# VectorE's order from pair 10 on, and second MLP steps in one piece, in an attention-then-MLP kernel on one core

## The chip, the core and the metric

The kernel runs on one core of a Trainium2 chip. A core has five engines with a queue of instructions each: TensorE (PE, matrix products), VectorE (DVE), ScalarE (ACT), GpSimd (POOL) and SyncE (SP, which here only issues DMAs). They wait for one another by semaphores; within an engine instructions run in the order of its queue. SBUF is the working memory of 128 partitions; PSUM holds TensorE's results, in banks. The metric is the device time of one execution in microseconds, lower is better.

## The reference, cut to what matters

```python
# q, k, v: (8 batches, 8 heads, 576 positions, 64); factor 4
q_d, k_d, v_d = means of q, k, v over groups of 4 positions      # 144 positions
out_d   = softmax(q_d k_d^T / 8) v_d                             # coarse attention
out_up  = out_d, each row repeated 4 times
out_loc = softmax(q k^T / 8 where |i - j| < 4) v                 # local attention
x = (out_up + out_loc) as (4608 tokens, 512)
h = x @ w_in                                                     # 512 -> 2048
out = (h * sigmoid(h)) @ w_out                                   # 2048 -> 512
```

## The kernel before

Attention runs over 32 pairs of heads (`NPAIR`), the MLP over 9 blocks `j` of 512 tokens. Each piece of work is a *unit* with a name, an engine and an estimated cost. A planner (`Plan.order`, L252) puts the units of each engine in order: first those that are written out by hand in `FIRST` (L164), then, whenever an engine is free in its model, the ready unit with the lowest priority value. A unit made without a priority gets its number in order of making.

For one pair p the units are:

- `T{p}` (PE, L600): transposes q and k into the PSUM banks o0 and pe_. `eq{p}` copies q out of o0 (`qT`, ScalarE up to pair 11, VectorE from 12 on, L396), `ek{p}` copies k out of pe_ (ScalarE, L616), `mk{p}` and `mq{p}` make the sums over 4 positions (VectorE, L620 and L624).
- `S{p}` (PE, L636): scores into bank pair AB. `x{p}` and `xd{p}` (ScalarE, L658 and L660) take the exponentials; `x{p}` also releases later loads of q, k and v on SP (`tick`). `k{p}` (VectorE, L662) multiplies by the band mask.
- `Z{p}` (PE): row sums into CD. `r{p}` (VectorE, three instructions, L771, L772, L774) adds the two halves and takes reciprocals; `z{p}` and `b{p}` (DMAs issued by ScalarE, L776 and L779) send them to HBM and back, spread as `Rb`.
- `PV{p}` (PE): products with v into CD. `m{p}` (VectorE, four instructions, L809 to L812) multiplies by `Rb` into `xo`; `a{p}` (GpSimd, L836) adds coarse and local parts into `xT`, the MLP's input.
- GpSimd also casts what is loaded: `va`, `cw`, `vb`, `c` (L593, L588, L595, L578).

From pair 10 on, T of pair n+1, S of pair n, PV of n-2 and Z of n-1 are one TensorE unit, `V{n}` (L902).

The MLP has two kinds of steps. `g1_{j}_{f}` (L841) is 4 matmuls into one half of bank pair HP; `t{j}_{f}` (ScalarE, tanh, L850) and `s{j}_{f}` (VectorE, L852) make 128 columns of the gated hidden layer `gT` of it and free the half. `g2_{j}_{tt}_{part}` (L858) is 4 of the 16 matmuls that make 128 rows of the output in o0 or pe_; after part 3, `o{j}_{tt}` (ScalarE, L867) copies them out and SP stores them. So bank o0 is shared: T writes it, `eq` reads it, then g2 writes it, `o` reads it, and T of the next step follows.

The last loop (L986) makes one `V`, four g1 and one g2 of four parts a step; from there on the planner's choice follows priorities, as `FIRST` ends in the steps V10 to V12.

Of the kernel before, what the change touches and what calls it, by code (L numbers as in the profile page):

```python
# [15 lines left out]
NPAIR = B_ * H_ // 2  # L16
# [3 lines left out]
NDIR = 10  # L20
# [131 lines left out]
class Unit:  # L152
# [5 lines left out]
    def __init__(self, eng, name, cost, prio, dcost=0.0):  # L158
# [7 lines left out]
        T0 T1 S0 T2 S1 Z0 VP0 T3 Z1 RB0 PV0 VP1 S2 T4 PV1 RB1 Z2 VP2 S3 T5 PV2 Z3 RB2 VP3 S4 T6 PV3 RB3 Z4  # L166
        VP4 S5 T7 Z5 RB4 VP5 PV4 g1_0_0 g1_0_1 S6 T8 g1_0_2 g1_0_3 RB5 Z6 g1_0_4 S7 g1_0_5 PV5 VP6 g1_0_6
        RB6 T9 Z7 g1_0_7 g1_0_8 S8 PV6 VP7 g1_0_9 g1_0_10 RB7 T10 Z8 g1_0_11 g1_0_12 S9 PV7 VP8 g1_0_13
        g1_0_14 RB8 g1_0_15 g1_1_0 g1_1_1 V10 g1_1_2 g1_1_3 VP9 g2_0_0_0 g2_0_0_1 g2_0_0_2 RB9 g2_0_0_3
        g1_1_4 g1_1_5 V11 g1_1_6 g1_1_7 VP10 g2_0_1_0 g2_0_1_1""",  # L170
    "ACT": """
        lkx lk0 ckx eq0 ek0 cw0 eq1 ek1 cw1 x0 xd0 eq2 ek2 x1 xd1 ev0 rh0 eq3 ek3 eb0 rh1 ev1 x2 xd2 eq4 ek4
        eb1 rh2 ev2 x3 xd3 eq5 ek5 eb2 rh3 ev3 x4 xd4 eq6 ek6 eb3 rh4 ev4 x5 xd5 eq7 ek7 eb4 rh5 ev5 t0_0
        t0_1 x6 xd6 eq8 t0_2 t0_3 eb5 ek8 rh6 t0_4 x7 xd7 t0_5 ev6 t0_6 eb6 eq9 ek9 rh7 t0_7 t0_8 x8 xd8 ev7
        t0_9 t0_10 eb7 eq10 ek10 rh8 t0_11 t0_12 x9 xd9 ev8 t0_13 t0_14 eb8 t0_15 t1_0 t1_1 eq11 ek11 rh9
        t1_2 t1_3 x10 xd10 ev9 eb9 o0_0 t1_4 t1_5 ek12 x11 z10 t1_6 t1_7 xd11""",
    "DVE": """
        const const.1 const.2 const.3 const.4 const.5 const.6 const.7 const.8 const.9 const.11 const.10
        const.12 const.14 const.13 const.15 const.16 const.17 const.18 const.19 const.20 const.21 const.22
# [2 lines left out]
        mk2 r0 k1 rx0 rm0 rl0 r1 mk3 m0 rx1 rm1 rl1 k2 r2 mk4 rx2 m1 rm2 k3 rl2 r3 mk5 m2 rx3 rm3 rl3 k4 r4  # L182
        mk6 rx4 m3 rm4 k5 rl4 r5 mk7 rx5 m4 rm5 rl5 s0_0 s0_1 k6 mq8 s0_2 r6 s0_3 mk8 rx6 s0_4 rm6 k7 rl6 m5
        s0_5 s0_6 r7 mq9 mk9 rx7 s0_7 rm7 s0_8 rl7 k8 m6 s0_9 s0_10 r8 mq10 mk10 rx8 s0_11 rm8 s0_12 rl8 k9
        m7 s0_13 s0_14 s0_15 s1_0 s1_1 r9 m8 mk11 rx9 s1_2 rm9 s1_3 rl9 mq11 k10 s1_4 s1_5 r10 eq12 mk12
        mq12 s1_6""",
    "POOL": """
        const.28 const.31 const.29 const.32 const.30 const.33 const.34 const.35 const.36 const.66 const.69
        const.42 const.43 const.44 const.45 const.46 const.47 const.48 const.49 const.50 const.51 const.52
        const.53 const.54 const.55 const.56 const.57 const.58 const.59 const.60 const.61 mq0 c2 mq1 c3 mq2  # L190
        cw2 c4 w0 cw3 mq3 c5 a0 cw4 mq4 w1 c6 a1 cw5 mq5 a2 w2 c7 cw6 mq6 a3 c8 cw7 w3 a4 mq7 c9 cw8 w4 c10
        w5 a5 w6 cw9 w7 a6 a7 c11 cw10 c12 cw11 cw12 c13 a8 a8.1 a8.2 c14 cw13""",
    "SP": """
        lq0 lq1 lk1 lv0.1 lv0.2 lv0.3 lq2 lv0e lv0 lk2 lv1 lv1.1 lv1.2 lv1.3 lq3 lk3 lv2 lv2.1 lv2.2 lv2.3
        lq4 lk4 lv3 lv3.1 lv3.2 lv3.3 lq5 lk5 lv4 lv4.1 lv4.2 lv4.3 lq6 lk6 lv5 lv5.1 lv5.2 lv5.3 lq7 lk7
        lv6 lv6.1 lv6.2 lv6.3 lq8 lk8 lv7 lv7.1 lv7.2 lv7.3 lq9 lk9 lv8 lv8.1 lv8.2 lv8.3 lq10 lk10 lv9
        lv9.1 lv9.2 lv9.3 lq11 lk11 lv10 lv10.1 lv10.2 lv10.3 lv11 lv11.1 lv11.2 lv11.3 lq12 lk12 lq13 lk13
        lv12 lv12.1 lv12.2 lv12.3 lq14 lk14 lv13 lv13.1 lv13.2 lv13.3 out0_0 lq15 lk15 lv14 lv14.1 lv14.2""",
}

class Plan:
# [109 lines left out]
def bass_hourglass_attn__then__act_silu_kernel(  # L311
# [9 lines left out]
    with kctx:  # L321
        E = kctx.enter_context
        L = Plan()
        res = {}

        def R(name, psum=False):
            if name not in res:
                res[name] = Res(name, psum)
            return res[name]
# [57 lines left out]
        def one(eng, name, cost, fn, r=(), w=(), dma=None, prio=None, dcost=0.0):  # L387
            u = L.unit(eng, name, cost, prio, dcost)
            L.op(u, fn, r, w, dma)
            return u  # L390
# [4 lines left out]
        def copy(eng, e, out_, in_):  # L395
            return e.activation(out_, in_, AF.Copy) if eng == "ACT" else e.tensor_copy(out_, in_)  # L396
# [3 lines left out]
        def half(j):  # L400
            return slice(64 * j, 64 * j + 64)
# [195 lines left out]

        def pe_T(u, p):  # L600
            a, b = p % NB, (p - 1) % NB
            for r in range(9):
                for j, h, x, t, n in ((0, 0, 0, o0, a), (0, 1, 1, pe_, a), (1, 1, 0, o0, a), (1, 0, 1, pe_, b)):
                    o = t[half(h), 0:288].bitcast(BF16)[:, 64 * r:64 * r + 64]
                    w = qkb[n][half(j), x, 64 * r:64 * r + 64]
                    L.op(u, lambda e, o=o, w=w, j=j: e.transpose(o, w, idn[half(j), :]),  # L606
                         [R("id"), R(f"qkb{n}{x}")], [rE if x else rF])

        def after_T(p):
            j = p % NT  # L610
            eng = "ACT" if p < NEQ else "DVE"
            one(eng, f"eq{p}", 0.68 if p < NEQ else 0.72, lambda e: copy(
                eng, e, qT[j][:, :].rearrange("p (g r) -> p g r", r=9),
                o0[:, 0:288].bitcast(BF16).rearrange("p (r g) -> p g r", r=9)),
                r=[rF], w=[R(f"qT{j}")])
            one("ACT", f"ek{p}", 0.68, lambda e: e.activation(  # L616
                kT[j][:, 3:579].rearrange("p (g r) -> p g r", r=9),
                pe_[:, 0:288].bitcast(BF16).rearrange("p (r g) -> p g r", r=9), AF.Copy),
                r=[rE], w=[R(f"kT{j}")])
            one("DVE", f"mk{p}", 0.74, lambda e: e.tensor_reduce(  # L620
                kd[j][:, 0:SD], kT[j][:, 3:579].rearrange("p (g r) -> p g r", r=4), AX.X, ALU.add),
                r=[R(f"kT{j}")], w=[R(f"kd{j}")])
            if p >= NMQ:
                one("DVE", f"mq{p}", 0.74, lambda e: e.tensor_reduce(  # L624
                    qd[j][:, :], qT[j][:, :].rearrange("p (g r) -> p g r", r=4), AX.X, ALU.add),
                    r=[R(f"qT{j}")], w=[R(f"qd{j}")])
                return
            half_ = vt[:, :, :].rearrange("p a b -> p (a b)")[:, 0:288].rearrange("p (g r) -> p g r", r=2)
            q4 = qT[j][:, :].rearrange("p (g r) -> p g r", r=4)
            u = L.unit("POOL", f"mq{p}", 1.2)  # L630
            L.op(u, lambda g: g.tensor_tensor(half_, q4[:, :, 0:2], q4[:, :, 2:4], ALU.add),
                 r=[R(f"qT{j}")], w=[R("vt")])
            L.op(u, lambda g: g.tensor_tensor(qd[j][:, :].unsqueeze(2), half_[:, :, 0:1], half_[:, :, 1:2], ALU.add),
                 r=[R("vt")], w=[R(f"qd{j}")])
# [49 lines left out]
        def acc(p):  # L684
            return (HP, rH) if p < 4 and p % 2 else (CD_, rCD_)
# [67 lines left out]
        def after_Z(p):  # L753
            i, u = p % 2, p % NR
            CD, rCD = acc(p)
            if p < NDIR:
                (h, m, l), rp = [rpart[p % 2][:, k, :] for k in range(3)], rpr[p % 2]
                zs, rest, rz = zr[i][:, :], rrest[p % 2][:, :], R(f"rrest{p % 2}")
                sg = [R("sgn0"), R("sgn1")]
                one("DVE", f"r{p}", 0.56, lambda e: e.reciprocal(zs, CD[:, 0, 360:432]), r=rCD[:1], w=[R(f"zr{i}")],  # L760
                    prio=-400000)
                one("ACT", f"rh{p}", 0.25, lambda e: e.activation(h, zs, AF.Copy), r=[R(f"zr{i}")], w=[rp[0]],
                    prio=-400000)
                one("DVE", f"rx{p}", 0.2, lambda e: e.scalar_tensor_tensor(  # L764
                    rest, h, sgn[:, 0:1], zs, ALU.mult, ALU.add), r=[R(f"zr{i}"), rp[0]] + sg, w=[rz], prio=-400000)
                one("DVE", f"rm{p}", 0.15, lambda e: e.tensor_copy(m, rest), r=[rz], w=[rp[1]], prio=-400000)
                one("DVE", f"rl{p}", 0.2, lambda e: e.scalar_tensor_tensor(
                    l, m, sgn[:, 1:2], rest, ALU.mult, ALU.add), r=[rz, rp[1]] + sg, w=[rp[2]], prio=-400000)
                return
            q = L.unit("DVE", f"r{p}", 0.9, -400000)  # L770
            L.op(q, lambda e: e.tensor_copy(zr[i][:, :], CD[:, 0, 432:504]), rCD[:1], [R(f"zr{i}")])  # L771
            L.op(q, lambda e: e.tensor_tensor(zr[i][:, :], zr[i][:, :], CD[:, 1, 432:504], ALU.add),  # L772
                 [R(f"zr{i}"), rCD[1]], [R(f"zr{i}")])
            L.op(q, lambda e: e.reciprocal(zr[i][:, :], zr[i][:, :]), [R(f"zr{i}")], [R(f"zr{i}")])  # L774
            eng = "ACT"
            dma(eng, f"z{p}", scr[u][0:74, :], zr[i][0:74, :], [R(f"scr{u}")], f"scr{u}", 0.2, r=[R(f"zr{i}")], prio=-500000)  # L776
            for h in range(2):
                src = bass.AP(tensor=scr[u].tensor, offset=scr[u].offset + 64 * h * 72, ap=[[0, 64], [1, 720]])
                dma(eng, f"b{p}", Rb[u][half(h), :], src, [R(f"Rb{u}{h}")], f"Rb{u}{h}", 0.85,  # L779
                    r=[R(f"scr{u}")], prio=-500000)  # L780
# [17 lines left out]
        def after_PV(p):  # L798
            u, x = p % NR, p % NX
            CD, rCD = acc(p)  # L800
            q = L.unit("DVE", f"m{p}", 0.92 if p < NDIR else 1.4, -450000 if L.boost else None)
            rb, wx = Rb[u][:, :].rearrange("p (x n) -> p x n", x=2), [R(f"xo{x}")]
            rr = [R(f"Rb{u}0"), R(f"Rb{u}1")]
            if p < NDIR:
# [148 lines left out]
        def G1(n):  # L953
            for _ in range(n):
                if todo:
                    g1(*todo.pop(0))

        def G2(parts):
            j, tt = todo2[0]
            u = 4 * j + tt  # L960
            bank, rb = (o0, rF) if u < 22 or u % 2 else (pe_, rE)
            for p in parts:
                g2(j, tt, p, bank, rb)
            if parts[-1] == 3:
                todo2.pop(0)
# [20 lines left out]
        while todo or todo2:  # L986
            if n < NPAIR + 2:
                V(n)
                if n <= NDIR:
                    RB(n - 1)  # L990
                if n <= NVP:
                    VP(n - 1)
                feed()
            G1(1)
            G2((0,))
            G1(1)
            G2((1,))
            G1(1)
            G2((2, 3))
            G1(1)  # L1000
            n += 1
        P = Prog()
        for u in L.order({"PE": 14, "ACT": 40, "DVE": 40, "POOL": 30, "SP": 40}, FIRST):
# [36 lines left out]
```

## Time and profile before

| what | value |
|---|---|
| median of 3 runs | 358.88 us (358.0, 358.88, 358.92) |
| the profiled execution | 358.17 us, of it a span of 356.4 us from the first to the last instruction |
| mean granted TensorE clock in it | 0.976 |
| start of V10, V14, V15, V16 | 74.5, 109.0, 118.7, 127.9 us |
| start of V31 | 257.9 us |

How to read it: times count from the start of the span. "PEld" is TensorE's loading of weights, which overlaps its matmuls. A row of the timeline gives start, duration, engine, line, operation, what is written from what, and, in brackets, how long the engine stood idle before and what ended that; "issue" there means that nothing the profile shows was waited for. ACTq and SPq are the queues of these engines when they issue DMAs. Consecutive instructions of one kind are merged into one row with their count. Some records of matmuls are missing from a trace.

### The profile page before, as it was taken

The numbers are of one execution on the slowest core, as the hardware profiler recorded it, in microseconds if no ns is written. First come the engines' busy times: TensorE is split into PE (matmuls) and PEld (weight loads), VectorE is DVE, ScalarE is ACT, GpSimd is POOL, SyncE is SP. The second block draws the span as 40 slices with busy tenths as digits, with TensorE's granted clock in tenths as the row PEclk, the third lists the DMA queues.
The fourth block names the chain that finished last, engine by engine and source line by source line (L and its number), as shares of the span: only waits on it lengthen the run. The fifth ranks groups of instructions, "written<-read, shape, count | busy, mean of one in ns | idle before, by whom it ended". The sixth has DMA issues, their size and how long they took to land.

```text
span 356.4 us, 11922 instructions
## 1 busy us (share of the span) xinstructions
PE 326.5 (92%) x5108; PEld 212.4 (60%) x5138; DVE 251.5 (71%) x502; ACT 179.1 (50%) x326; POOL 156.3 (44%) x203
## 2 busy tenths in 40 slices
PE   0593799899999999999999999999999999999996
PEld 0472677666665666666666666666665666666642
DVE  7487879877788889888899988988866534343400
ACT  2775568766554454545554555555543343434321
POOL 7786875262464736475556665664111100000000
PEclk9997589999999999999999999999999999999999
DMA  8999999956878797877888888763222000110012
GB/s 230 239 257 240 290 298 234 208 157 196 224 209 231 207 224 212 228 218 212 219 233 217 221 218 229 209 175 95 77 92 86 31 29 29 51 39 29 31 59 88
DMA packets 73510, 60.34 MB, mean 169 GB/s; under 512 B 47986, under 2 KB 55794, under 8 KB 73458
## 3 DMA queue, kind: packets, MB, share of 16 engines
q1 hardware_dynamic: 63818, 44.27, 46.9%
q10 hardware_dynamic: 5416, 9.02, 8.9%
q0 software_dynamic: 4224, 6.29, 8.3%
q8 instruction: 40, 0.66, 0.8%
q14 instruction: 12, 0.10, 0.1%
HBM read 51.76 MB, written 9.91 MB: 173 GB/s over the span
## 4 chain that ended last, share of the span: by engine, by line
PE 84%; DVE 5%; ACT 3%; DMA 2%; issue 2%; SPq 2%; ACTq 0%; DVEq 0%
PE HP L393 38%; PE o L393 27%; PE pe_ L393 8%; PE CD L393 5%; PE AB L393 4%; SPq L498 2%; PE o L606 2%; DMA vs<-in_v_dram 1%; DVE rrest L764 1%; DMA scr<-zr 1%; DVE gT L852 1%; ACT th L850 1%; DVE kd L620 1%; PE pe_ L606 1%; ACT osb L867 1%
## 5 line engine op out<-in xcount | busy, mean ns | idle before, releaser
L393 PE MATMUL HP<-xT,w_in_sb 128*128 128x512 f32 x576 | 165.7, 423 | 0.9 <-DVE gT L852 0.9
L852 DVE SCALAR_TENSOR_TENSOR gT<-th,HP 128x512 bf16<-128x512 f32 x144 | 96.6, 683 | 66.3 <-ACT th L850 65.8
L850 ACT ACTIVATE th<-HP 128x512 f32<-128x512 f32 x144 | 84.2, 598 | 114.1 <-PE HP L393 91.3
L393 PEld LDWEIGHTS HP<-xT,w_in_sb 128*128 128x128 f32 x576 | 106.7, 190 | 28.8 <-DVE gT L852 1.3
L393 PE MATMUL o<-w_out_bf,gT 128*128 128x512 bf16 x437 | 104.1, 380 | 2.6
L393 PEld LDWEIGHTS o<-w_out_bf,gT 128*128 128x128 bf16 x464 | 41.3, 98 | 55.9 <-issue 8.5
L836 POOL TENSOR_TENSOR xT<-xo 128x576 fp32r<-128x576 f32 (+3 forms) x48 | 44.5, 939 | 60.3 <-DVE xo L812 46.1
L593 POOL TENSOR_TENSOR vt<-vq 128x512 f32<-128x512 f32 x18 | 23.0, 1276 | 44.6 <-DMA vq<-in_v_dram 44.6
L578 POOL CAST qkb<-qk 128x1152 bf16<-128x1152 f32 x30 | 34.7, 1156 | 8.1 <-PE pe_ L606 3.7
L867 ACT ACTIVATE osb<-o 128x512 f32<-128x512 f32 x29 | 17.3, 597 | 24.8 <-PE o L393 24.7
L606 PE MATMUL o<-idn,qkb 64*64 64x64 bf16 x576 | 17.6, 203 | 9.9 <-DVE qkb L573 6.3
L393 PE MATMUL pe_<-w_out_bf,gT 128*128 128x512 bf16 x109 | 26.1, 380 | 0.2
L588 POOL CAST vb<-vs 128x640 bf16<-128x640 f32 x30 | 21.7, 724 | 7.4 <-DMA vs<-in_v_dram 7.4
L620 DVE TENSOR_REDUCE kd<-kT 128x144 bf16<-128x576 bf16 x32 | 23.5, 734 | 1.1 <-ACT kT L616 1.0
L616 ACT ACTIVATE kT<-pe_ 128x576 bf16<-128x576 bf16 x32 | 21.0, 655 | 2.4 <-PE pe_ L606 0.6
L658 ACT ACTIVATE Pt<-AB 128x576 bf16<-128x576 f32 x32 | 20.7, 646 | 0.9 <-PE AB L393 0.8
L606 PEld LDWEIGHTS o<-idn,qkb 64*64 64x64 bf16 x576 | 14.0, 118 | 10.3 <-DVE qkb L573 6.3
L606 PE MATMUL pe_<-idn,qkb 64*64 64x64 bf16 x576 | 16.5, 204 | 2.8 <-DVE qkb L575 2.1
L393 PEld LDWEIGHTS pe_<-w_out_bf,gT 128*128 128x128 bf16 x112 | 10.0, 98 | 13.6 <-issue 3.2
L624 DVE TENSOR_REDUCE qd<-qT 128x144 bf16<-128x576 bf16 x24 | 17.8, 742 | 0.0
L812 DVE TENSOR_TENSOR xo<-CD,Rb 128x576 f32<-128x576 f32 x22 | 16.7, 757 | 0.8
L660 ACT ACTIVATE Pd<-AB 128x432 bf16<-128x432 f32 x32 | 17.0, 532 | 0.0
(85 smaller groups left out, 356.2 us busy)
## 6 DMA issues: line engine op xcount, KB each, us to landing
vs<-in_v_dram SPq DMA_DIRECT2D x126, 80.0 KB, 4.2
qk<-in_q_dram SPq DMA_DIRECT2D x32, 288.0 KB, 3.7
out_dram<-osb SPq DMA_DIRECT2D x36, 256.0 KB, 2.7
qk<-in_k_dram SPq DMA_DIRECT2D x30, 288.0 KB, 4.7
Rb<-scr ACTq DMA_DIRECT2D x44, 180.0 KB, 4.1
vq<-in_v_dram SPq DMA_DIRECT2D x18, 256.0 KB, 4.7
w_in_sb<-in_moe_w_in_dram POOLq DMA_DIRECT2D x4, 1024.0 KB, 9.3
w_out_bf<-in_moe_w_out_dram POOLq DMA_DIRECT2D x4, 512.0 KB, 11.6
```

The source lines that it names most:

```text
L393: L.op(u, lambda t: t.matmul(out_, lhsT, rhs, start=start, stop=stop, skip_group_check=True), r, w)
L578: one("POOL", f"c{p}", 1.15, lambda g: g.tensor_copy(qkb[j][:, :, :], qk[i][:, :, :]), r=[R(f"qk{i}0"), R(f"qk{i}1")], w=[R(f"qkb{j}0"), R ...
L588: one("POOL", f"cw{p}", 0.72, lambda g: g.tensor_copy(vb[m][:, :, :], vs[i][:, :, :]), r=rr, w=[R(f"vb{m}")])
L593: one("POOL", f"va{p}", 1.3, lambda g: g.tensor_tensor(vt[:, :, :], vq[i][:, :, 0:128], vq[i][:, :, 128:256], ALU.add), r=rr, w=[R("vt")])
L606: L.op(u, lambda e, o=o, w=w, j=j: e.transpose(o, w, idn[half(j), :]), [R("id"), R(f"qkb{n}{x}")], [rE if x else rF])
L616: one("ACT", f"ek{p}", 0.68, lambda e: e.activation(kT[j][:, 3:579].rearrange("p (g r) -> p g r", r=9), pe_[:, 0:288].bitcast(BF16).rearra ...
L620: one("DVE", f"mk{p}", 0.74, lambda e: e.tensor_reduce(kd[j][:, 0:SD], kT[j][:, 3:579].rearrange("p (g r) -> p g r", r=4), AX.X, ALU.add), ...
L658: one("ACT", f"x{p}", 0.66, lambda e: e.activation(Pt[m][:, :, :], AB[:, :, 0:288], AF.Exp, scale=0.125), r=rAB, w=[R(f"P{m}"), R(f"tick{p ...
L836: one("POOL", f"a{p}", 0.15 + n * 0.0019, lambda g, dst=dst, in0=in0, in1=in1: g.tensor_tensor(dst, in0, in1, ALU.add), r=[R(f"xo{x}")], w ...
L850: one("ACT", f"t{j}_{f}", 0.62, lambda e: e.activation(th[tb][:, :], hps[hb], AF.Tanh, scale=0.5), r=[rH[hb]], w=[R(f"th{tb}")], prio=-1)
L852: one("DVE", f"s{j}_{f}", 0.71, lambda e: e.scalar_tensor_tensor(gT[j % 2][:, f, :], th[tb][:, :], 1.0, hps[hb], ALU.add, ALU.mult), r=[rH ...
L867: one("ACT", f"o{j}_{tt}", 0.62, lambda e: e.activation(osb[s_][:, :], bank[:, :], AF.Copy, scale=0.5), r=[rb], w=[R(f"osb{s_}")], prio=-3)
```

## The change

Four edits. `r{p}` of pairs from 10 on gets the number of `eq{p+2}` plus 0.5 as its priority, and no longer the lowest of all: it comes right after that q copy. `m{p}` gets its own number plus 8.5. In the last loop the order of a step is the first part of g2, two g1, the other three parts, two g1; it was g1, part 0, g1, part 1, g1, parts 2 and 3, g1. And `FIRST` is cut off on every engine near V10 to V11.

```diff
@@ FIRST: the ends of the five lists @@
-        g1_0_14 RB8 g1_0_15 g1_1_0 g1_1_1 V10 g1_1_2 g1_1_3 VP9 g2_0_0_0 g2_0_0_1 g2_0_0_2 RB9 g2_0_0_3
-        g1_1_4 g1_1_5 V11 g1_1_6 g1_1_7 VP10 g2_0_1_0 g2_0_1_1""",
+        g1_0_14 RB8 g1_0_15 g1_1_0 g1_1_1 V10 g1_1_2 g1_1_3 VP9 g2_0_0_0 g2_0_0_1 g2_0_0_2 RB9""",
...
-        t1_2 t1_3 x10 xd10 ev9 eb9 o0_0 t1_4 t1_5 ek12 x11 z10 t1_6 t1_7 xd11""",
+        t1_2 t1_3 x10 xd10 ev9""",
...
-        m7 s0_13 s0_14 s0_15 s1_0 s1_1 r9 m8 mk11 rx9 s1_2 rm9 s1_3 rl9 mq11 k10 s1_4 s1_5 r10 eq12 mk12
-        mq12 s1_6""",
+        m7 s0_13 s0_14 s0_15 s1_0 s1_1 r9 m8 mk11 rx9 s1_2 rm9 s1_3 rl9 mq11""",
...
@@ after_T @@
+            eqi[p] = len(L.units)
             one(eng, f"eq{p}", 0.68 if p < NEQ else 0.72, lambda e: copy(
@@ after_Z @@
-            q = L.unit("DVE", f"r{p}", 0.9, -400000)
+            q = L.unit("DVE", f"r{p}", 0.9, eqi[p + 2] + 0.5 if p + 2 < NPAIR else None)
@@ after_PV @@
-            q = L.unit("DVE", f"m{p}", 0.92 if p < NDIR else 1.4, -450000 if L.boost else None)
+            q = L.unit("DVE", f"m{p}", 0.92 if p < NDIR else 1.4, -450000 if L.boost else len(L.units) + 8.5)
@@ the last loop @@
-            G1(1)
             G2((0,))
-            G1(1)
-            G2((1,))
-            G1(1)
-            G2((2, 3))
-            G1(1)
+            G1(2)
+            G2((1, 2, 3))
+            G1(2)
```

What the planner makes of it, for the step of V18, in the order of each queue:

| engine | before | after |
|---|---|---|
| PE | V18 g1 g1 g2(0,1,2) g1 g2(3) g1 | V18 g1 g1 g2(0,1,2,3) g1 g1 |
| DVE | r17 eq19 mk19 mq19 s s m16 k18 s s | eq19 r17 s s mk19 mq19 k18 m16 s s |
| ACT | ek19 x18 z17 t t xd18 b17 b17 t o t | ek19 x18 t t z17 xd18 o t b17 b17 t |

This order holds from about V16 to V30. POOL's order changes in one place near the end, SP's not at all. In V11, V12 and V14 both b of a step stand after `o` and ahead of the last two t in the new kernel; before, they stood ahead of `o`. In V12 and V13 VP comes between the two g1 that follow V, where it came after them. At V31 to V33 one part of g2 stands on the other side of V. Up to VP9 the orders are the same, and so are those of the stretch after V33 apart from the pairing of g1 and g2 parts.

More of the change, by code (lines that the diff above doesn't have):

```diff
@@ L191 @@
         cw2 c4 w0 cw3 mq3 c5 a0 cw4 mq4 w1 c6 a1 cw5 mq5 a2 w2 c7 cw6 mq6 a3 c8 cw7 w3 a4 mq7 c9 cw8 w4 c10
-        w5 a5 w6 cw9 w7 a6 a7 c11 cw10 c12 cw11 cw12 c13 a8 a8.1 a8.2 c14 cw13""",
+        w5 a5 w6 cw9 w7 a6 a7 c11 cw10 c12 cw11 cw12 c13 a8 a8.1 a8.2""",
     "SP": """
@@ L197 @@
         lv9.1 lv9.2 lv9.3 lq11 lk11 lv10 lv10.1 lv10.2 lv10.3 lv11 lv11.1 lv11.2 lv11.3 lq12 lk12 lq13 lk13
-        lv12 lv12.1 lv12.2 lv12.3 lq14 lk14 lv13 lv13.1 lv13.2 lv13.3 out0_0 lq15 lk15 lv14 lv14.1 lv14.2""",
+        lv12 lv12.1 lv12.2 lv12.3 lq14 lk14 lv13""",
 }
@@ L596, in castv @@
                 vd[m][:, :, :], vt[:, :, 0:64], vt[:, :, 64:128], ALU.add), r=[R("vt")], w=[R(f"vd{m}0"), R(f"vd{m}1")])
+        eqi = {}
         def pe_T(u, p):
```

## Prediction

> **What bounds the kernel now.** I read the page first: its span, the busy sums, the slices.
>
> ```profile
> span 356.4 us, 11922 instructions
> PE 326.5 (92%) x5108; PEld 212.4 (60%) x5138; DVE 251.5 (71%) x502; ACT 179.1 (50%) x326; POOL 156.3 (44%) x203
> PE   0593799899999999999999999999999999999996
> DVE  7487879877788889888899988988866534343400
> ```
>
> TensorE is at 9 in nearly every slice from the ninth on; VectorE is at 8 to 9 up to slice 29 and falls to 3 or 4 after it. A busy TensorE need not be at its peak, so I went to the timeline of one step, the one of V25 (a "step" is one pass of the last loop, and V25 its unit of attention matmuls).
>
> ```profile
> 205.91 0.35 PE L393 MATMUL AB<-qT,kT 64*64 64x58 bf16 x20
> ...
> 207.13 2.14 PE L393 MATMUL HP<-xT,w_in_sb 128*128 128x512 f32 x8
> 207.26 0.65 ACT L658 ACTIVATE Pt<-AB 128x576 bf16<-128x576 f32 x1
> 207.28 0.23 DVE L771 COPY zr<-CD 128x72 f32<-128x72 f32 x1
> ...
> 208.40 0.69 DVE L396 COPY qT<-o 128x576 bf16<-128x576 bf16 x1
> ...
> 209.15 2.27 PEld L393 LDWEIGHTS o<-w_out_bf,gT 128*128 128x128 bf16 x12 [0.32 <-DVE qT L396]
> ...
> 211.48 1.13 ACTq L498 DMA_DIRECT2D Rb<-scr  x2
> 211.52 0.30 DVE L809 COPY xo<-CD 128x144 f32<-128x144 f32 x1
> ...
> 212.69 0.55 PEld L393 LDWEIGHTS o<-w_out_bf,gT 128*128 128x128 bf16 x4 [0.28 <-issue]
> ...
> 213.36 0.61 DVE L662 TENSOR_TENSOR Pt<-Pt,mask_bf 128x576 bf16<-128x576 bf16 x1
> ...
> 214.59 0.35 PE L393 MATMUL AB<-qT,kT 64*64 64x58 bf16 x20
> ```
>
> The step takes 214.59 - 205.91 = 8.68 us, and the steps V16 to V30 all take 8.63 to 8.68. V takes 1.22 of it (to the first HP matmul). The other 32 matmuls start 0.23 (HP) or 0.216 us (o) apart. So nearly nothing is left in a step. The wait that the change aims at is the one marked "<-DVE qT": the first second-MLP matmul writes the bank that the q copy (L396) must read first. Its price is small: with the wait the weight loads idle 0.32, at the same turn without it 0.27 ("<-issue"). The view of waits gives the same over the whole run: 5.2 us in 16 waits against 8.5 us in 31 turns, 0.325 - 0.274 = **0.05 us a step**.
>
> Three rows of another step show what decides most of my forecast:
>
> ```profile
> 176.93 0.73 POOL L595 TENSOR_TENSOR vd<-vt 128x256 bf16<-128x256 f32 x1
> ...
> 177.60 1.31 DVE L811 TENSOR_TENSOR xo<-xo,Rb 128x144 f32<-128x144 f32 x1
> 177.61 1.13 POOL L578 CAST qkb<-qk 128x1152 bf16<-128x1152 f32 x1
> ```
>
> L811 has a median of 317 ns; here it took 1.31 us and ended 0.17 after GpSimd's cast did. All six L811 over 0.6 us end 0.16 or 0.17 after an instruction of GpSimd that reads SBUF, and all four mask products (L662) of 0.61 us in place of 0.45 that come after 100 us end 0.31 after it. VectorE's products of two SBUF operands wait for GpSimd's instruction to end; its copies, reductions and PSUM readers don't show this.
>
> **The change, part by part.** Times below count from the start of V.
>
> (a) q copy ahead of row sums, G2 in one piece. The q copy ends 1.1 us earlier (the row sums' L771, L772 and L774 take 1.12 from start to start), so the 0.05 goes: 16 x -0.05 = **-0.8**. Fewer turns between HP and o save nothing: in the last part 8 HP and 8 o matmuls with two turns take 284.43 to 288.01 = 3.58 us, and 8 x 0.2325 + 8 x 0.216 is 3.59.
>
> (b) V15. Before, its transposes wait for the drain of bank o at 118.83 to 119.42, which stood on ScalarE behind the two Rb issues (1.10 us at 117.19); the weight loads of the transposes idle 0.48 there. After, the drain stands ahead of those issues and two g1 lie before V15: **-0.5**. V14 has G2 right before it in both kernels and keeps its wait.
>
> (c) ScalarE's order. After, the two Rb issues stand between the last two tanh of a step (from V15 on). TensorE runs its 16 o matmuls from 3.20 to 6.65; the third g1's last matmul starts at 7.37, ends at 7.76; tanh 7.80 to 8.40; the issues take 1.10, to 9.54; only then the fourth tanh, 9.60 to 10.20, where its input was ready at 8.7 (at 118.34 a tanh starts 0.05 after such an issue ends, so the queue does hold it). The issue of zr to scr stands after the second tanh now, at 4.1 and not 2.6; it lands within 4 and so before 8.4, where Rb's issues come anyway. Its SwiGLU product (L852) runs from 10.24 to 10.92. With a step of 8.62 that is 1.62 to 2.30 of the next step. That product frees HP's second half for the second g1 of the next step, whose first matmul is due at 2.27. Release to weight load takes 0.05 (q copy to load, 209.10 to 209.15). Bounds of this new wait: 0.05, and 0.16 if the weight load isn't made ahead (the first HP matmul after V is followed after 0.34 in place of 0.23). I take 0.1 where nothing larger lies over it. In V12, V13 and V15 both last tanh stand behind the issues: the third product ends near 1.45 + 0.05 against 1.22 wanted, 0.25 each: **+0.75**.
>
> (d) What else that tanh holds up: kT copy, then the exponentials (L658), which begin at 2.2 and not 1.35. Their end releases the q, k and v loads on SP's queue (q's issue starts 0.02 after it), eight or nine issues in a row to about 7.8, and the last of them is what GpSimd's chain (L593, L588, L595, L578; 3.4 us without gap) waits for in the next step. So the chain comes about 0.8 later, less what a step grows: I take 0.7. Rb's loads go out 2.9 us later, 9.5, land some 4.1 later at 13.6 and are read at 16: covered by 2.4 us.
>
> (e) mask product and m. VectorE after: q copy 2.25, row sums 2.86, two products 3.98 and 4.58, reductions 5.18 and 5.84, mask product 6.48, m 6.85 to 8.72 (1.87 undisturbed), two products. Before, the mask product came after m, mostly behind GpSimd's chain; now it comes at 6.48, inside it. PV of the next step, 0.53 after its start, needs m (bank CD): m may end at 8.62 + 0.53 - 0.05 = 9.10. The first g1's bank, freed by the product after m, gives nearly the same limit (9.17). GpSimd's q/k cast ended, in V16 to V28, at 7.35, 6.54, 7.70, 6.55, 6.90, 7.52, 8.06, 7.38, 6.22, 7.75, 7.09, 6.65, 6.27; add 0.7 and call it E.
> Where the cast has begun by 6.48 (E under 7.62, six steps), the mask product ends at E + 0.31 and m at E + 2.1: over the limit by 0.24, 0.25, 0.60, 0, 0.35, 0 = 1.44.
> Where L595 runs at 6.48 (four), the mask product slips in before the cast, L811 waits for its end, m ends at E + 0.95: over by 0.05 in all. If it loses the boundary, as L811 did at 177.60 (those at 116.09 and 186.28 won), 1.0 each: 4 x 1/3 x 1.0 = 1.3.
> Where L588 runs (three), E + 0.95 again: 0.25, 0.60, 0.30 = 1.15.
> Sum 3.95. A step that grows brings the next chain earlier in its own count, so part of each wait is repaid by the next step; I keep seven tenths of the sum (an estimate: of two steps in a row over by 0.6, the second has E lower by 0.6 and no wait, while single ones keep theirs): 2.75. The five or so steps with no wait here pay (c)'s 0.1, and V29 and V30, without loads, too: 0.5 + 0.2. **+3.45**. Bounds: nothing (the chain not later, or the mask product always through) and 8 us (every boundary lost).
>
> The Trainium skill ("SBUF — State Buffer", "Who interferes with whom") says that an operation with two SBUF inputs and a GpSimd operation that reads SBUF exclude each other for the whole instruction, and that issue order decides. It speaks against putting the mask product here. By it a product that already waits would always go before the cast; the 177.60 row, issued 0.01 before the cast and yet last, doesn't agree. By the page (e) would be 0.7 x 1.3 = 0.9 smaller and the sum 360.5.
>
> (f) j changes. Where g1 goes on to the next 512 tokens (V18, V22, ...), its fourth matmul alone needs the newest pair, at 2.04; the addition (L836) starts 0.08 after m and takes 1.37: 8.72 + 1.45 - 8.62 = 1.55. Covered by 0.5; gone if m ends after 9.2, and then part of the same lateness. In V12 and V13 the values' projection (VP) moves between two g1, and in V31 to V33 V moves behind one part of a g2: the same matmuls with a turn more or less, which (a) priced at nothing. The last 80 us have the same matmuls in the same blocks.
>
> Sum: -0.8 - 0.5 + 0.75 + 3.45 = **+2.9**. The profiled execution took 358.17 (span 356.4 and 1.8 around it); the three runs shown have the median 358.88. I add to 358.5, the mean of all four: **361.4**.
>
> **Rivals.** R1, faster: the new waits aren't there (tanh and issues fall otherwise than counted, GpSimd's chain stays early), and (a) and (b) remain: 358.5 - 1.3 = 357.2. For it: (c) hangs on tenths; Rb's issues may leave the vq loads less company and so speed the chain. Against: the fourth tanh is late by 0.9 whatever the DMAs do. It decides where m ends before 9.1 in every step.
> R2, no change: (c) and a few of (e)'s waits, about 1.7 instead of 4.2, balance (a) and (b): 358.9. For it: half of the 13 steps have none in my count.
> R3, much slower: the mask product loses most boundaries and m's lateness feeds the two products after it, the tanh and the next chain; VectorE, at 17.6 to 18.6 busy of 20 us, has little to catch up with. 13 x 0.55 + 0.75 = +7.9: 366.4. Against: each wait of TensorE also gives VectorE time.
>
> **Chances.** Forecast 0.5 (own range 359.8 to 364.5), R1 0.2, R2 0.2, R3 0.1. The range 357.1 to 365.0 takes in most of R1 and R2 and leaves out R3. A measurement of this kernel tells about 0.3% (1.1 us) from no change; so faster 0.2, same 0.2, slower 0.6.
>
> **What would show it.** Right: no wait of o's weight loads on the q copy; steps V16 to V28 of unequal length, 8.65 to 9.3, V29 and V30 shorter; waits of CD on L812 or HP on L852; mask products of 0.6 us and more; Rb issues right ahead of the last tanh. Wrong: equal steps of 8.62 (R1), L662 at 0.45 throughout, or exponentials that still start at 1.35.

## The result, and the profile after

The changed kernel takes 358.55 us (median of 20 runs, 356.98 to 361.33) against 358.3 us for the kernel before (20 runs on the same chips, 355.42 to 362.41): a ratio of 1.0014, 95% interval 0.9989 to 1.0038. That is no change that can be measured. (This ratio and those below leave out runs more than 1.5% above the fastest of their kernel, so they are not the quotients of the medians.) The forecast was 361.4; the time lies inside its range, the forecast of "slower" does not hold.

The page of the profiled execution (359.22 us): span, busy sums, and VectorE's forty slices.

```profile
span 357.5 us, 11952 instructions
PE 331.0 (93%) x5138; PEld 217.4 (61%) x5138; DVE 253.2 (71%) x502; ACT 181.5 (51%) x326; POOL 153.9 (43%) x203
DVE  7584889977788799898888888898866443434310
```

The span is 1.1 us longer. The starts of the V units say where (before, then after):

| stretch | before | after | difference |
|---|---|---|---|
| start to V10, ahead of everything changed | 74.50 | 74.93 | +0.43 |
| V10 to V15 | 44.19 | 44.52 | +0.33 |
| V15 to V16 | 9.19 | 8.89 | -0.29 |
| V16 to V30, 14 steps | 121.39 | 122.29 | +0.91 |
| V30 to the end | 107.16 | 106.83 | -0.33 |

The first row is chance: over the eleven profiles of the experiments V10 starts at 73.0 to 76.4 us. The +0.33 of the second row is 0.20 in V12 and V13, 0.21 in V10 and V11 and -0.08 in V14; V10 and V11 together take 18.4 to 18.6 in the profiles that have the new order there. The row to explain is the 14 like steps: 8.67 each before, 8.67 to 8.79 after.

The timeline of V25's step after (start, duration, engine, line, what is written from what):

```profile
206.26 0.60 ACT L851 ACTIVATE th<-HP 128x512 f32<-128x512 f32 x1 [0.26 <-PE HP L391]
206.27 1.12 ACTq L496 DMA_DIRECT2D Rb<-scr  x2
...
207.07 0.35 PE L391 MATMUL AB<-qT,kT 64*64 64x58 bf16 x20
...
207.44 0.60 ACT L851 ACTIVATE th<-HP 128x512 f32<-128x512 f32 x1 [0.58 <-PE HP L391]
...
207.63 0.36 PEld L391 LDWEIGHTS CD<-Pt,vb 64*64 64x64 bf16 x20
...
208.42 2.11 PE L391 MATMUL HP<-xT,w_in_sb 128*128 128x512 f32 x8
...
208.54 0.65 ACT L659 ACTIVATE Pt<-AB 128x576 bf16<-128x576 f32 x1
...
213.12 0.45 DVE L663 TENSOR_TENSOR Pt<-Pt,mask_bf 128x576 bf16<-128x576 bf16 x1
...
213.18 1.39 POOL L576 CAST qkb<-qk 128x1152 bf16<-128x1152 f32 x1
...
214.26 0.48 DVE L812 TENSOR_TENSOR xo<-xo,Rb 128x144 f32<-128x144 f32 x1
214.77 0.76 DVE L813 TENSOR_TENSOR xo<-CD,Rb 128x576 f32<-128x576 f32 x1
215.76 0.35 PE L391 MATMUL AB<-qT,kT 64*64 64x58 bf16 x20
```

Three things are to be seen. The Rb issues (ACTq) start 0.01 after a tanh starts and run beside it; they don't wait for its end, so the last tanh starts at 207.44 = V+0.37, not at V+0.98. The products L812 and L813 end at 215.53, 8.46 after V's start and under the limit of 9.10 that the forecast's step (e) gives for them. And V itself, from its first AB matmul to its first HP matmul, now takes 208.42 - 207.07 = 1.35 and not 1.22.

The same through groups, over 128 to 249 us, which holds 14 steps in each kernel; after the bar stand busy us, mean ns of one, and idle time with what ended it. Before:

```profile
L593 POOL TENSOR_TENSOR vt<-vq 128x512 f32<-128x512 f32 x14 | 17.8, 1272 | 36.8 <-DMA vq<-in_v_dram 36.8
L811 DVE TENSOR_TENSOR xo<-xo,Rb 128x144 f32<-128x144 f32 x14 | 8.5, 609 | 1.9
L393 PEld LDWEIGHTS CD<-Pt,vb 64*64 64x64 bf16 x280 | 3.7, 106 | 0.0
```

After:

```profile
L591 POOL TENSOR_TENSOR vt<-vq 128x512 f32<-128x512 f32 x14 | 18.0, 1286 | 19.2 <-DMA vq<-in_v_dram 19.0 <-POOL xT L837 0.2
L663 DVE TENSOR_TENSOR Pt<-Pt,mask_bf 128x576 bf16<-128x576 bf16 x14 | 8.6, 613 | 0.0
L391 PEld LDWEIGHTS CD<-Pt,vb 64*64 64x64 bf16 x280 | 5.2, 103 | 0.2
L812 DVE TENSOR_TENSOR xo<-xo,Rb 128x144 f32<-128x144 f32 x13 | 4.2, 321 | 1.7
```

GpSimd waits 19.2 us for the v loads in place of 36.8: its chain comes earlier, not later. L812 costs 321 ns and no longer 609. And the 280 weight loads of V's products take 5.2 us together in place of 3.7, (5.2 - 3.7) / 14 = 0.11 a step, though one takes no longer (103 ns): there is a pause between them. In V16 to V30 each V has one, 82 to 141 ns long (V17's is split in two), which ends at V+0.69 to V+0.72; no semaphore wait stands there, and the matmul that it falls on differs (the second to the seventh of the group). Before, no V from V16 on has one.

### The profile page after: what moved, and what is told of

The parts are those of the page before. It is cut to its first block, busy times and chain, and to the rows that moved or that the text cites. A ratio compares the mean times of both kernels' runs of the same rounds, so it can differ in the third digit from the quotient of the medians.

```text
span 357.5 us, 11952 instructions
## 1 busy us (share of the span) xinstructions
PE 331.0 (93%) x5138; PEld 217.4 (61%) x5138; DVE 253.2 (71%) x502; ACT 181.5 (51%) x326; POOL 153.9 (43%) x203
## 4 chain that ended last, share of the span: by engine, by line
PE 84%; DVE 7%; DMA 2%; SPq 2%; ACT 2%; issue 2%; ACTq 0%; DVEq 0%
PE HP L391 36%; PE o L391 27%; PE pe_ L391 8%; PE CD L391 6%; PE AB L391 4%; SPq L496 2%; DMA scr<-zr 2%; PE o L606 1%; DVE rrest L765 1%; DVE xo L806 1%; DVE rp L767 1%; DVE gT L853 1%; DMA vs<-in_v_dram 1%; DVE rp L768 1%; ACT th L851 1%
## 5 line engine op out<-in xcount | busy, mean ns | idle before, releaser
L391 PE MATMUL HP<-xT,w_in_sb 128*128 128x512 f32 x576 | 156.8, 413 | 2.1 <-DVE gT L853 1.9
L853 DVE SCALAR_TENSOR_TENSOR gT<-th,HP 128x512 bf16<-128x512 f32 x144 | 97.3, 678 | 64.3 <-ACT th L851 63.7
L851 ACT ACTIVATE th<-HP 128x512 f32<-128x512 f32 x144 | 85.9, 598 | 70.8 <-PE HP L391 69.2
L391 PE MATMUL o<-w_out_bf,gT 128*128 128x512 bf16 x464 | 106.3, 380 | 0.0
L837 POOL TENSOR_TENSOR xT<-xo 128x576 fp32r<-128x576 f32 (+3 forms) x48 | 41.4, 877 | 80.5 <-DVE xo L813 68.0
L391 PEld LDWEIGHTS o<-w_out_bf,gT 128*128 128x128 bf16 x464 | 42.8, 98 | 54.5 <-issue 7.2
L663 DVE TENSOR_TENSOR Pt<-Pt,mask_bf 128x576 bf16<-128x576 bf16 x32 | 17.5, 546 | 0.7 <-ACT Pt L659 0.7
L813 DVE TENSOR_TENSOR xo<-CD,Rb 128x576 f32<-128x576 f32 x22 | 16.7, 757 | 0.8
```

The costliest lines, as they stand in the source:

```text
L391: L.op(u, lambda t: t.matmul(out_, lhsT, rhs, start=start, stop=stop, skip_group_check=True), r, w)
L837: one("POOL", f"a{p}", 0.15 + n * 0.0019, lambda g, dst=dst, in0=in0, in1=in1: g.tensor_tensor(dst, in0, in1, ALU.add), r=[R(f"xo{x}")], w ...
L851: one("ACT", f"t{j}_{f}", 0.62, lambda e: e.activation(th[tb][:, :], hps[hb], AF.Tanh, scale=0.5), r=[rH[hb]], w=[R(f"th{tb}")], prio=-1)
L853: one("DVE", f"s{j}_{f}", 0.71, lambda e: e.scalar_tensor_tensor(gT[j % 2][:, f, :], th[tb][:, :], 1.0, hps[hb], ALU.add, ALU.mult), r=[rH ...
```

## The experiments

Three theories of the pause were put up: A, the late last tanh; B, the Rb issues, whose second ends at V+0.31; C, TensorE's own instruction stream in its new order. Most edits only rewrite one engine's order (the lists of `FIRST` written out to the end), for pairs 14 to 29 where nothing else is said; the diffs show one step of it. The table has, for each run, the 14 steps from V16 to V30, the time from V to its first HP matmul, the mean time after V's start at which GpSimd's q/k cast ends (V16 to V28), and the ratio to the kernel before where it was timed. The mean granted clock of the profiles is 0.970 to 1.000 and does not enter: the undisturbed step of the changed order is 8.607 in a profile at 0.971 and 8.606 in one at 1.000.

| kernel | V16-V30 | V | cast ends | ratio, 95% |
|---|---|---|---|---|
| before | 121.39 | 1.22 | 7.07 | |
| after | 122.29 | 1.32-1.43 | 6.01 | 1.0014 [0.9989, 1.0038] |
| 1 issues after the drain | 121.92 | 1.25, some 1.27-1.76 | 7.18 | 0.9986 [0.9953, 1.0018] |
| 2 the same, tanh late | 121.39 | 1.25, three 1.39-1.78 | 6.65 | |
| 3 before, issues late | 125.19 | 1.28-1.36 | 5.70 | 1.0123 [1.0093, 1.0153] |
| 4 last tanh at V+0.98 | 123.07 | 1.31-1.44, one 1.25 | 6.86 | 1.0037 [1.0011, 1.0063] |
| 5 issues from SyncE | 121.65 | 1.25-1.54 | 6.87 | |
| 6 another source for Rb | 122.16 | 1.31-1.40 | 6.78 | |
| 7 issues behind the exponentials | 120.49 | 1.25 | 5.65 | 0.9923 [0.9893, 0.9952] |
| 8 mask product early too | 120.49 | 1.25 | 6.05 | 0.9923 [0.9892, 0.9953] |
| 9 before, issues behind the exponentials | 121.38 | 1.22 | 5.76 | 0.9999 [0.9963, 1.0035] |
| 10 before, g2 in one piece | 121.95 | 1.22, one 1.42 | 7.29 | 0.9992 [0.9959, 1.0025] |
| 11 before, VectorE's priorities | 123.29 | 1.25-1.60 | 5.93 | 1.0053 [1.0010, 1.0096] |

**1. The issues ahead of both last tanh.**

```diff
 ACT, V19's step
-xd19 o2_1 t3_6 b18 b18 t3_7 ek21 x20
+xd19 o2_1 b18 b18 t3_6 t3_7 ek21 x20
```

> The changed kernel with the two Rb issues of V16 to V31's steps moved ahead of both last tanh, right behind the drain of o (ScalarE: o, b, b, tanh, tanh; every other engine as it is). The last tanh then starts at V+0.11 as in V12 and V13, and no issue lies inside V. Theory A (the last tanh lying over V at V+0.35 makes TensorE pause) and theory B (the issues that end at V+0.31, or their transfers, make it pause): V falls from 1.33-1.43 to 1.25 us in steps V16 to V30, steps of 8.56 to 8.60, the time 2 to 2.4 us under the changed kernel's: about 356.3, ratio to the kernel before 0.994 to 0.997. Theory C (the pause comes from TensorE's own stream and waits in the new order): V stays at 1.33-1.43, steps 8.73, ratio 1.000 to 1.002.

The pause is gone wherever the second issue ends before V-0.1, and where nothing else holds TensorE V takes 1.25 and the step 8.607, as theories A and B said. But the time is not 2 us lower. Six of the 14 steps stand at 8.63 to 9.11, 1.43 us over the rest in all (V26 and V27 have a late issue and a pause besides). The timeline of V23's end and V24:

```profile
194.19 1.15 POOL L576 CAST qkb<-qk 128x1152 bf16<-128x1152 f32 x1
194.21 1.45 DVE L663 TENSOR_TENSOR Pt<-Pt,mask_bf 128x576 bf16<-128x576 bf16 x1
...
195.18 0.60 ACT L868 ACTIVATE osb<-o 128x512 f32<-128x512 f32 x1 [2.51 <-PE o L391]
...
195.90 1.11 ACTq L496 DMA_DIRECT2D Rb<-scr  x2
...
196.68 0.76 DVE L813 TENSOR_TENSOR xo<-CD,Rb 128x576 f32<-128x576 f32 x1
196.86 0.24 PEld L391 LDWEIGHTS AB<-qT,kT 64*64 64x64 bf16 x20 [0.36 <-issue]
...
197.06 1.08 ACT L851 ACTIVATE th<-HP 128x512 f32<-128x512 f32 x2 [1.28 <-PE HP L391]
...
197.69 1.29 DVE L853 SCALAR_TENSOR_TENSOR gT<-th,HP 128x512 bf16<-128x512 f32 x2 [0.25 <-ACT th L851]
...
198.43 1.68 PEld L391 LDWEIGHTS HP<-xT,w_in_sb 128*128 128x128 f32 x8 [0.32 <-DVE gT L853]
```

Two things meet here. The mask product is issued 0.02 after the cast and takes 1.45; L813 ends at 197.44, 9.33 after V23's start and past the limit of step (e). But that is not what holds HP for 0.32. The SwiGLU product L853 starts 0.25 after L813 has ended, when the tanh is ready, and the tanh stands behind the Rb issues, which start 0.72 after the drain of o and not beside it. They wait for the reciprocals: the store to scr was issued at 191.85 and landed 4.03 later, and Rb's first issue starts 0.02 after that. It is the same ahead of V23 and V26 (landed 4.05 and 4.28 after the issue; at most 3.6 where Rb's issue starts beside the drain); ahead of V27 the second issue takes 1.30 in place of 0.62. These late issues make about 1.4 of the 1.43 us.

Step (e) of the forecast is a real mechanism all the same: in V18 and V24 the load of CD waits for L813, with gaps of 0.11 and 0.07, and V18's step is 0.05 longer for it. It needs a late chain, and with the issues back at their early place the cast ends at 7.18 again; even so it costs little here.

The Trainium skill ("SBUF — State Buffer", "Who interferes with whom") lets issue order decide which of the two waits. These rows agree: here the cast was first and the product took 1.45; at 213.12 above the product was first, took 0.45, and the cast 1.39 in place of 1.15. The row at 177.60 of the kernel before did not.

**2. The last tanh late, without an issue near it.** A copy that nothing reads stands ahead of it.

```diff
+one("ACT", f"D{n}", 0.25, lambda e: e.activation(rrest[0][:, :], rrest[1][:, :], AF.Copy), ...)
 ACT
-o2_1 b18 b18 t3_6 t3_7
+o2_1 b18 b18 t3_6 D20 t3_7
```

> The first experiment (issues ahead of both last tanh) with a small ScalarE copy of 128x72, whose result nothing reads, between the last two tanh, so that the last one starts near V+0.35 again while no issue is there. Theory A (the late tanh): V at 1.35 or more as in the changed kernel, with a gap near V+0.6. Theory B (the issues): V at 1.25 without the gap. Theory C: V as in the first experiment.

The copy came out too early for its purpose: the last tanh starts mostly at V+0.15. But it starts at V+0.51 in V16, V+0.28 in V18 and V+0.66 in V25, and none of these V has a pause. The only one of this run is in V27, where the second issue came late and ended at V+0.36; the pause ends at V+0.76. That speaks against theory A; run 4 settles it.

**3. The kernel before, with the issues at the turn of the step.**

```diff
 ACT, V19's step of the kernel before
-z18 t3_4 t3_5 xd19 b18 b18 t3_6 o2_1 t3_7
+z18 t3_4 t3_5 xd19 t3_6 o2_1 b18 b18 t3_7
```

> The kernel before with ScalarE's order alone changed: the two Rb issues stand behind the drain of o and ahead of the last tanh (tanh, o, b, b, tanh), so that they end near V+0.3 and the last tanh starts near V+0.35; TensorE, VectorE, GpSimd and SyncE keep their order. Theories A and B: V grows from 1.22 to 1.33-1.43 and the steps V16 to V30 from 8.66 to about 8.8, +2 us, ratio 1.005 to 1.007. Theory C: V stays at 1.22 and the ratio within 0.998 to 1.003.

Rows of V25's step:

```profile
208.34 1.10 ACTq L498 DMA_DIRECT2D Rb<-scr  x2
209.07 0.24 PEld L393 LDWEIGHTS AB<-qT,kT 64*64 64x64 bf16 x20 [0.36 <-ACT osb L867]
...
209.63 0.40 PEld L393 LDWEIGHTS CD<-Pt,vb 64*64 64x64 bf16 x20
209.66 0.48 PE L393 MATMUL CD<-Pt,vb 64*64 64x58 bf16 x20
210.14 1.29 POOL L593 TENSOR_TENSOR vt<-vq 128x512 f32<-128x512 f32 x1 [0.53 <-DMA vq<-in_v_dram]
```

With TensorE's order untouched the pause is there, in all 15 V: theory C falls too, B holds. L593 starts at V+1.07 here, at V+3.95 in V25 of the kernel before, and the cast ends at 5.70: moving the Rb issues alone brings the chain 1.4 us forward. The run is slower than expected, since the late tanh also makes the first VectorE work of the step late, and the wait on the q copy, which this kernel still has, grew from 5.2 to 7.6 us (0.15 a step).

**4. The last tanh where the forecast had put it.**

```diff
+one("ACT", f"D{n}", 0.6, lambda e: e.activation(dum[:, :], w_in_sb[:, 0, 0:512].bitcast(F32), AF.Copy), ...)
 ACT
-t3_6 b18 b18 t3_7
+t3_6 b18 b18 D20 t3_7
```

> The changed kernel with a ScalarE copy of 128x512 (0.6 us, its result read by nothing) ahead of the last tanh of V16 to V31's steps, so that this tanh starts near V+0.98, where the forecast had put it. If only the forecast's count of tanh and issues was wrong, and its later steps hold (exponentials at V+2.2, GpSimd's chain later by 0.7, mask products of up to 1.3 us behind it, m ending after V+9.1): steps of 8.65 to 9.3 with waits of CD on VectorE, and a time some 2.5 to 3.5 us over the changed kernel's, ratio to before 1.007 to 1.011. If the later steps were wrong as well (GpSimd's chain is not tied to the exponentials as I counted, m keeps under its limit): no wait of CD on VectorE, only HP's 0.1 a step, at most +1.5 over the changed kernel, ratio 1.001 to 1.006.

The last tanh starts at V+0.9, and the pause stays where it was, ending at V+0.68 to V+0.74 in eleven of the 15 V: theory A falls. In V18, V24 and V28 the load of CD waits for L813 instead, with gaps of 0.28, 0.09 and 0.14: part of what step (e) feared. The cast ends 0.85 later than in the changed kernel, as step (d) reckons, but from 6.01, and so at 6.86. Thirteen steps take 8.68 to 8.81, the pauses and these waits included, 8.73 in the mean, as the 14 of the changed kernel; one of 9.53 (V22) has its issue itself held up (1.48 in place of 0.62) and ScalarE's queue behind it, and makes the whole 0.8 us by which the 14 steps are longer. The ratio is 0.0023 over the changed kernel's, with intervals that overlap. Most of the later waits do not come even at this place of the tanh.

**5. and 6. Who issues, and what is read.** In 5, SyncE issues both; in 6, they read other rows.

```diff
-dma(eng, f"b{p}", Rb[u][half(h), :], src, ...)
+dma("SP" if 13 < p < 30 else eng, f"b{p}", Rb[u][half(h), :], src, ...)
```

> The changed kernel with the two Rb issues of pairs 14 to 29 made by SyncE, ahead of the out store, in place of ScalarE. The last tanh starts at V+0.11 and ScalarE issues nothing near V. If it is ScalarE's queue that makes TensorE pause: V takes 1.25 without a gap. If it is Rb's transfer, whoever issues it: a gap in V whose end is 0.40 us after the end of the second issue wherever that lies inside V (issue ends from about V+0.4 to V+0.9), V at 1.33 or more in those steps.

```diff
-src = bass.AP(tensor=scr[u].tensor, offset=scr[u].offset + 64 * h * 72, ap=[[0, 64], [1, 720]])
+src = bass.AP(tensor=k.tensor, offset=k.offset + 64 * h * 720, ap=[[720, 64], [1, 720]])
```

> The changed kernel with another source for the two Rb transfers of pairs 14 to 29: 64 different rows of 2880 bytes of the input k in place of 64 times the same row of scr, so the reciprocals of these pairs are not applied; shape, size, place and waits are the same. If TensorE pauses because 64 descriptors read the same address: V 1.25 without a gap. If issue and size are what counts: the gap stays, ending 0.40 after the second issue, V 1.33 to 1.43.

Rows of 5, V25's step:

```profile
204.06 1.12 SPq L496 DMA_DIRECT2D Rb<-scr  x2
204.69 0.24 PEld L391 LDWEIGHTS AB<-qT,kT 64*64 64x64 bf16 x20 [0.36 <-ACT th L851]
...
205.26 0.26 PEld L391 LDWEIGHTS CD<-Pt,vb 64*64 64x64 bf16 x20
...
205.43 0.35 PEld L391 LDWEIGHTS CD<-Pd,vd 64*64 64x64 bf16 x8
```

The issue ends at 205.18 = V+0.49; the gap is now behind the vb group, among the eight loads of vd, and ends at V+0.88, 0.39 later. Over this run second issues that end at V+0.39, 0.49, 0.62, 0.70 and 0.76 have gaps that end at 0.78, 0.88, 1.01, 1.09 and 1.14. Two first issues, ending at V+0.61 and V+0.70, have a gap of 88 ns each, ending at 0.99 and 1.09. (The gaps of V28 and V29, 0.38 and 0.10, are waits of CD for L813.) So it is not ScalarE's queue. In 6 the gap is where it was: not the reading of one address either. Stores of the output issued at such times have none (in V21 of run 5 one ends at V+0.71).

**7. The issues behind the exponentials** of the next step, where ScalarE waits for the first g1 anyway (pairs 12 to 29).

```diff
 ACT
-o2_1 t3_6 b18 b18 t3_7 ek21 x20 t3_8 t3_9
+o2_1 t3_6 t3_7 ek21 x20 b18 b18 t3_8 t3_9
```

> The changed kernel with the two Rb issues (of pairs 12 to 29) moved to the next step, right behind its exponentials: from V+1.4 to V+2.5, where ScalarE waits for the first g1 anyway; no other engine's order changes. Theory B (what makes TensorE pause is the second Rb issue, 0.4 us before the pause's end): the pause falls at V+2.8 among the long HP matmuls and costs nothing, V takes 1.25, steps 8.61, 2 us under the changed kernel, ratio to before 0.993 to 0.997. GpSimd's chain: if Rb's transfers hold up the v loads, as the two runs with them early and late suggest (c ends at 7.1 to 7.2 with them issued ahead of V's end, at 5.7 to 6.0 with them issued at the turn of the step), it now ends at about 6; if they hold up the q and k loads as well, at 6.5 to 7.5, with mask products up to 1.4 us and some steps 0.1 to 0.5 longer. Against: Rb may land too late for L812 (landing is 4 us after the issue, L812 comes 5.2 after it), then L812 waits on it and m runs over V+9.1.

Rows of V25's step, and two groups over 128 to 249 us:

```profile
205.75 0.60 ACT L851 ACTIVATE th<-HP 128x512 f32<-128x512 f32 x1 [0.32 <-PE HP L391]
206.20 0.26 PEld L391 LDWEIGHTS CD<-Pt,vb 64*64 64x64 bf16 x20
...
206.47 1.18 ACTq L496 DMA_DIRECT2D Rb<-scr  x2
206.88 1.68 PEld L391 LDWEIGHTS HP<-xT,w_in_sb 128*128 128x128 f32 x8
...
207.01 0.65 ACT L659 ACTIVATE Pt<-AB 128x576 bf16<-128x576 f32 x1
...
212.73 0.31 DVE L812 TENSOR_TENSOR xo<-xo,Rb 128x144 f32<-128x144 f32 x1
```

```profile
L591 POOL TENSOR_TENSOR vt<-vq 128x512 f32<-128x512 f32 x14 | 18.1, 1292 | 16.0 <-DMA vq<-in_v_dram 16.0
L391 PEld LDWEIGHTS CD<-Pt,vb 64*64 64x64 bf16 x280 | 3.7, 106 | 0.0
```

The vb group is back at 3.7 us, Rb is there in time for L812 (0.31 in all steps), all 14 steps take 8.606 or 8.607, and the kernel is faster than both: ratio 0.9923. The interval is 1.7 to 3.8 us; from V10 on the profiles differ by 1.6 us (280.3 against 281.9), a little less.

**8. The mask product early, and V14's wait.**

```diff
 DVE
-eq21 r19 s3_6 s3_7 mk21 mq21 k20 m18
+eq21 k20 r19 s3_6 s3_7 mk21 mq21 m18
 PE
-g1_1_14 VP12 g1_1_15 g2_0_3_0 ... g2_0_3_3 V14
+g1_1_14 VP12 g2_0_3_0 ... g2_0_3_3 g1_1_15 V14
```

> The run with the issues behind the exponentials, and two edits more: VectorE's mask product right behind the exponentials (ahead of the row sums, at V+2.05, when GpSimd's chain has mostly not begun), and the last g1 ahead of V14 put behind G2, so that V14's transposes need not wait for the drain of bank o. If the mask product under GpSimd's cast is what still makes single steps long, no wait of CD on VectorE is left, every step from V16 on takes 8.61; V14's wait of 0.6 goes: 2.5 to 3.5 us under the changed kernel, ratio to before 0.990 to 0.995. Rival: row sums, reciprocals and so z's issue come 0.45 later and hold ScalarE's queue, or Rb comes too late: ratio 0.996 or more.

The 14 steps are the same 8.607, so the mask product had no cost left to give; V14's step falls from 9.76 to 9.40. The ratio cannot be told from run 7's.

**9. The kernel before with run 7's move.**

```diff
 ACT, V19's step of the kernel before
-xd19 b18 b18 t3_6 o2_1 t3_7 ek21 x20
+xd19 t3_6 o2_1 t3_7 ek21 x20 b18 b18
```

> The kernel before with ScalarE's order alone changed: the two Rb issues of pairs 12 to 29 moved behind the next step's exponentials, as in the run of the changed kernel with the same move. It tells what the change itself is worth once the place of these issues is the same in both. If the change is worth what its own wait was (the q copy's 0.05 a step, the turn and one piece 0.03) this kernel's steps take 8.65 to 8.67 against 8.607, V 1.22: some 0.9 us more over V16 to V30 than the changed kernel with the move, ratio to before 0.996 to 1.001. If most of the gain of that run came from the move and not from the change (GpSimd's chain at 5.7 and not 7.1, no boundary with it), steps of 8.60 to 8.62 here too, ratio 0.991 to 0.995.

Steps of 8.67 as before, with the cast at 5.76: in these steps of this kernel an early chain is worth nothing. The ratio of 0.9999 tells less, with its interval of 0.7% (the medians of all runs are 358.11 and 359.12). So what run 7 gains in the 14 steps is the change's own, and the issues' place only let it be seen: (121.38 - 120.49) / 14 = 0.064 a step. It is a net figure, as V itself takes 1.25 there and 1.22 here. Not all of run 7's 1.6 us is the change's: from V10 on run 9 takes 281.4, as the move alone shortens V15's step from 9.18 to 8.67.

**10. and 11. Each part alone.** 10 has the edit of the last loop, 11 those of the two priorities, both with `FIRST` as long as it was.

```diff
 10
-G1(1) G2((0,)) G1(1) G2((1,)) G1(1) G2((2, 3)) G1(1)
+G2((0,)) G1(2) G2((1, 2, 3)) G1(2)
 11
-r{p}: -400000      m{p}: -450000 if L.boost else None
+r{p}: eqi[p + 2] + 0.5 if p + 2 < NPAIR else None      m{p}: -450000 if L.boost else len(L.units) + 8.5
```

> The kernel before with one part of the change alone: the second MLP step in one piece (G2 whole between two pairs of g1), VectorE's priorities as they were (row sums ahead of the q copy, m ahead of the mask product). By the forecast turns cost nothing and the wait on the q copy stays: same as before within 0.3%, ratio 0.998 to 1.002; ScalarE then issues Rb ahead of o's drain, far from V, so no pause: V 1.22, steps 8.62 to 8.67. Rival: with both last tanh behind G2 the product of the last one comes late for the next step's second g1, HP waits: ratio 1.003 or more.

> The kernel before with the other part of the change alone: VectorE's priorities of row sums and m lowered (q copy ahead of row sums, mask product ahead of m), the second MLP step in its three pieces between single g1. No wait of o's weight loads on the q copy: -0.8 in all by the forecast's first term. In this order the pairs' units lie between other g1, so the last tanh and the Rb issues stand elsewhere: where the second issue ends between V-0.1 and V+0.8 a pause of 0.1 in V is due 0.4 later. If only the first term counts: ratio 0.996 to 0.999. If the issues' place counts: steps with a pause 0.13 longer than those without, ratio 0.999 to 1.004.

The one piece alone is no change: eleven of the 14 steps take 8.63 to 8.68, V16, V20 and V28 take 8.74 to 9.14. VectorE's priorities alone are slower: here the planner also moves TensorE's units, long steps stand beside short ones (V17 7.81, V18 10.90), and eleven of 15 V have a pause that ends 0.37 to 0.41 after the end of an issue. That run mixes several causes, and its ratio is not put down to one.

## Why the prediction was wrong

- **(a), -0.05 a step: right.** No load of o waits for the q copy after the change, and with the pauses away the step is 8.607 where 8.62 was forecast. The turns saved little, as said.
- **(b), V15 -0.5: right.** The wait for the drain is gone; that step is 0.29 shorter, and 0.58 shorter in run 7. The 0.30 between them is a wait of (c)'s kind: at 121.00 HP's weight load has idled 0.26 for the SwiGLU product, because the Rb issues ahead of both last tanh started 0.71 after the drain of o. They waited for the reciprocals, which landed 5.36 after the issue of their store.
- **(c), the fourth tanh at V+0.98: wrong.** The two issues were counted after the third tanh; they run beside it. The tanh starts at V+0.35. Of the +0.75 of V12, V13 and V15 only V15's came, and by that late landing, not by the count: runs 1, 4 and 6 have the same order there, and the step takes 8.59 to 8.61. V12 and V13 have no such wait. They are 0.20 longer in all, and stay so in run 7, with the values' projection between two g1, which (f) priced at nothing (run 8, without it there, has V13's step 0.07 shorter).
- **(d), the chain 0.7 later: wrong in sign, and this is the step that failed.** The cast ends at 6.01 and not at 7.07, so the chain comes 1.1 earlier. That loads hang on the exponentials holds (run 4: 0.85 later than after). But the issues that move carry transfers, and these had run among the v loads: in V18 of the kernel before, Rb's packets run from 1.9 before V to 2.1 after it. Away from there the chain is 1.3 to 1.4 us earlier at once, with no other edit (runs 9 and 3). In V17 to V27 the last v load's issue ends 0.2 later after the change than before, but L593 starts 2.9 after it and no longer 4.1 (run 9: 3.2, run 3: 2.6). So the place of the issues is shown to be the cause; that the transfers crowd one another is the likely way, not shown by itself. The forecast named this under R1 and gave it no price.
- **(e), +2.75: not there.** It was built on a cast at 7.8 (7.07 + 0.7). With the cast at 6.01 m ends at 8.49 in the mean. Three mask products do wait (1.33, 1.25 and 0.99 in V16, V18 and V27), but L813 ends at 9.12 at the latest and no load of CD waits. The mechanism is real, with gaps of up to 0.11 in run 1 and 0.28 in run 4; what it would cost with a cast at 7.8 no run shows.
- **R2's time came, but not by R2.** That the measured time lies inside the range is luck. What eats the gain is in no term of the sum: the pause in V, which with its surroundings costs (122.29 - 120.49) / 14 = 0.13 a step, 1.8 us, against the 0.9 that the change earns there. The records of before could not show it, since there the issue ended some 2 us ahead of V. A chance of 0.2 for "same" was too low for a sum whose largest term hung on tenths.

## What to carry to other kernels

When a moved step issues DMAs, ask first what their transfers leave and what they join; here that moved GpSimd's chain by 1.1 us one way, where the waits of the moved instructions were counted at 0.7 the other way. And ask what an issue itself waits for: one that waits for a landing holds up all that stands behind it in its engine's queue. A DMA issue doesn't stop the activation that runs already, so count it beside that one and ahead of the next. And where a gain of 0.06 a step vanishes, compare the inside of a unit that was not changed: the loss was there.

## What the runs showed of the hardware

TensorE pauses for about 0.1 us, ending some 0.4 us after the end of an Rb issue (64 rows of 2880 bytes), whichever of two engines issues it, and whether it reads one row 64 times or 64 rows. It is seen where it falls into the later half of V, with small matmuls some 8 ns apart, and not among the long ones. It isn't the running transfer: before, Rb's packets ran right through V without a gap. Nor is it tied to their first packets: in V16 to V21 after the change these start at V+0.56 to V+0.86, and the pause ends at V+0.69 to V+0.71 each time. What holds TensorE is open. The Trainium skill ("SBUF — State Buffer", "Who interferes with whom") has DMAs on ports of their own that no compute engine shares; the packets through V agree with that. No run here shows whether the pause has to do with these ports.
